# A spectral mixer with a gated FFN on one core: the head's chain, the weight sums and the order of the steps rewritten

## The chip, the cores and the metric

The kernel runs on one core of a Trainium2 chip. The time is device microseconds of one launch. The core has five engines that run side by side, each in its own program order, and wait for each other by semaphores: TensorE (PE: matmuls, with PEld for the loading of weights), VectorE (DVE), ScalarE (ACT), GpSimd (POOL) and SyncE (SP), whose queue issues most transfers.

## The reference

x is 2048 x 512, all in fp32, with F = 1376:

```python
xn = _layernorm(x, axis=-1)
s = irfft2(rfft2(xn) * (w_r + 1j * w_i))      # the spectral filter, over both axes
gate, up = xn @ W_gate, xn @ W_up
g = silu((relu(gate) * up) @ W_down)
return x + s * g
```

## The kernel before

All heavy products run on PE in fp16. Each fp32 operand is split into a high and a low fp16 part, and a product is three passes: high by high, high by low, low by high. Before a weight is split, it is scaled by a power of two, one for each group of its 128-column tiles (`csc`), which is found from the sum of its squares. The split of a tile is an ACT pass (high = scale x raw) and a DVE pass (low = scale x raw - high). x^T, the transposed normalised rows, is split in the same way (`xT`).

**Stages.** The 2048 rows are eight chunks of two row tiles ("chunk c" below; row tiles 0 and 1 belong to chunk 0). Rows are loaded, normalised, transposed on PE ("turned"; tiles `head`), and go two ways: through the FFN in four blocks of 512 rows (gate and up products `gu`, hidden values `h`, down products `dn`), and through the transform (`fold`, the stages `s1`, `s2`, `y`, `z`, and so on). The last stage adds x + s * g and stores.

**The head.** While the first rows are on their way, PE runs idle matmuls into a PSUM tile `small` (`keep_busy`). The first rows' path is `load_x` (one transfer for each row tile of chunk 0), `stats` (bn_stats and bn_aggr on DVE), `deviation` (one over the standard deviation: DVE adds the epsilon, ACT takes a root of the variance, DVE takes the reciprocal and corrects it in one Newton step), `normalise` (`xf`), `turn_row` (four PE transposes into PSUM, a copy `xTf`, the high part of `xT` and its low part). The products of the first two weight groups (`product` with c = 0, f < 2) for the first two row tiles are made straight from fp32 `xTf` and `raw` weights, without a split; all others wait for split weights. Both row tiles of chunk 0 turn into one PSUM tile `head0`.

**Scales.** `squares` runs an ACT pass over each weight tile with a sum, `group_scale` adds the sums over the partitions with a small PE product (into `small` or `sum3`, `sum4`, ...) and makes the scale on DVE. Groups 3 to 5 are pairs of tiles.

**Weight sums.** For the later blocks, five pairs of weight tiles are multiplied in a scheme with fewer products, which needs sums and differences of scaled gate and up weights. `weight_sums` reloads the raw weights (`rp`), scales them in place on ACT (20 passes), makes four differences of each pair on DVE or POOL, and splits the results into high and low parts (`wT`, `wgu`).

**What sets the order.** Each piece of work is registered by `step` or `either` (a choice of engine), in the order of the code, with a cost and a due time. A table `ORDER` lists the number of the step to issue next, so it sets the order within every engine's queue; a string `PLACE` picks the engine of each step with a choice, and a string `SLOTS` the buffer of each tile. All instructions go out through the helper `InOrder`, so that nearly every row of the profile has that helper's line, L167 (L169 in the changed kernel), and instructions are told apart by their tiles.

Lines that the change touches: the constants at L40 to L48, the tables from L67, `load_x` L346, `stats` L362, `deviation` L373, `turn_row` L510, `squares` L616, `group_scale` L626, `all_scales` L673, `weight_sums` L680.

Of the kernel before, what the change touches and what calls it, by code (L numbers as in the profile page):

```python
# [42 lines left out]
NORM, TURN1 = (('DVE', 'DVE'), ('DVE', 'ACT')), 'PE'  # L43
# [3 lines left out]
BUSY, LATE = 42, 0.4  # L47
# [98 lines left out]
def columns(c, i):  # L146

    return (slice(0, 256), slice(256, 384), slice(384, D)) if (c, i) == (NBL - 1, 3) else (slice(0, D),)


def fwidth(f):
    return P if f < TAIL else F - P * TAIL


def fast(c, n):
    return c >= NBL - int(FASTS[n])


class InOrder:
# [77 lines left out]
def dve(n):  # L237
    return .07 + n / 960
# [27 lines left out]
def kernel(ctx: ExitStack, tc: tile.TileContext, x, wg, wu, wd, wl, ew, sp, c_r, c_d, c_m, c_x, c_s, out):  # L266
# [92 lines left out]
    def x_names(c, i):  # L359
        return [(f"x{c}", 0 if c else i)]  # L360
# [1079 lines left out]
```

## Time and profile before

| what | value |
| --- | --- |
| three runs | 397.18, 396.06, 395.64 us; median 396.06 |
| profiled execution | 394.64 us, of which 392.9 are the span of the trace |
| PE, DVE, ACT, POOL busy | 383.3, 312.0, 265.4, 92.0 us |
| PE's clock as granted | full speed over the whole span |
| first real product on PE | 9.36 us from the span's start |
| last product on PE ends | 386.75 us |

In a row of the timeline stand the start, the duration, the engine, the helper's line, the operation with what it writes and reads (the buffer numbers left out), the shapes and the count of the instructions that the row joins, and in brackets how long the engine was idle before it and which engine's result ended that. In a row of a group stand the count, then the busy time in us and the mean duration in ns, then the idle time in front of its instructions. "issue" and engine names with a q are the engine's sequencer.

### The profile page before, as it was taken

The numbers are of one execution on the slowest core, as the hardware profiler recorded it, in microseconds if no ns is written. First come the engines' busy times: TensorE is split into PE (matmuls) and PEld (weight loads), VectorE is DVE, ScalarE is ACT, GpSimd is POOL, SyncE is SP. The second block draws the span as 40 slices with busy tenths as digits, with TensorE's granted clock in tenths as the row PEclk, the third lists the DMA queues.
The fourth block names the chain that finished last, engine by engine and source line by source line (L and its number), as shares of the span: only waits on it lengthen the run. The fifth ranks groups of instructions, "written<-read, shape, count | busy, mean of one in ns | idle before, by whom it ended". The sixth has DMA issues, their size and how long they took to land. (4 is left out here: it accounts for less than half of the span.)

```text
span 392.9 us, 9009 instructions
## 1 busy us (share of the span) xinstructions
PE 383.3 (98%) x3548; PEld 264.5 (67%) x3548; DVE 312.0 (79%) x575; ACT 265.4 (68%) x517; POOL 92.0 (23%) x85
## 2 busy tenths in 40 slices
PE   8999999999999989999999999999999999999993
PEld 6865544545678868546888787745678776887543
DVE  5899999889798797996675997467475976369995
ACT  4989998899998976527648566644557654475511
POOL 2100023210250324320206225031114030432340
PEclk9999999999999999999999999999999999999999
DMA  7995377966476776898865606838556007999997
GB/s 272 402 344 189 114 185 176 313 156 141 140 262 191 285 202 186 215 203 206 270 236 171 208 2 203 238 78 196 139 171 193 13 7 206 261 238 271 235 231 192
DMA packets 67835, 77.97 MB, mean 198 GB/s; under 512 B 29072, under 2 KB 40944, under 8 KB 67792
## 3 DMA queue, kind: packets, MB, share of 16 engines
q1 hardware_dynamic: 66352, 74.77, 65.5%
q0 software_dynamic: 1440, 2.62, 4.4%
q8 instruction: 28, 0.46, 0.5%
q14 instruction: 15, 0.12, 0.1%
HBM read 46.95 MB, written 26.76 MB: 188 GB/s over the span
## 5 line engine op out<-in xcount | busy, mean ns | idle before, releaser
L167 PE MATMUL dn<-wds,h 128*128 128x512 f16 (+2 forms) x528 | 119.0, 372 | 0.0
L167 PEld LDWEIGHTS <-wgu 128*128 128x128 f16 x960 | 93.0, 98 | 38.3 <-issue 3.4
L167 PEld LDWEIGHTS <-h 128*128 128x128 f16 (+1 forms) x594 | 54.5, 98 | 51.5 <-issue 2.2
L167 PEld LDWEIGHTS <-wT 128*128 128x128 f16 x540 | 52.2, 98 | 9.8 <-issue 1.9
L167 PE MATMUL gu<-xT,wgu 128*128 128x512 f16 (+1 forms) x240 | 48.1, 358 | 0.8 <-DVE xT L167 0.8
L167 PE MATMUL sb<-xS,wT 128*128 128x256 f16 x360 | 44.2, 273 | 0.1
L167 PE MATMUL sa<-xT,wgu 128*128 128x256 f16 x360 | 44.2, 273 | 0.0
L167 PE MATMUL sb<-xS,wgu 128*128 128x256 f16 x180 | 22.1, 273 | 1.2 <-DVE se L167 1.2
L167 PE MATMUL sc<-xS,wgu 128*128 128x256 f16 x180 | 22.1, 273 | 0.0
L167 PE MATMUL sc<-xT,wT 128*128 128x256 f16 x180 | 22.1, 273 | 0.0
L167 ACT ACTIVATE g<-dn,cdi 128x512 f32<-128x512 f32 (+1 forms) x16 | 10.6, 671 | 12.7 <-PE dn L167 12.5
L167 POOL TENSOR_TENSOR h<-sr,h 128x512 f16<-128x512 f32 x8 | 10.2, 1280 | 31.6 <-ACT h L167 31.6
L167 PE MATMUL gu<-xT,wgt 128*64 128x256 f16 (+1 forms) x144 | 17.0, 309 | 0.0
L167 DVE TENSOR_TENSOR t<-v,t 128x1024 f16<-128x1024 f32 x8 | 9.8, 1223 | 8.5 <-ACT t L167 8.5
L167 ACT ACTIVATE p<-pf 128x1024 f16<-128x1024 f32 x8 | 8.5, 1058 | 11.9 <-DVE pf L167 8.7
L167 POOL TENSOR_TENSOR h<-se,h 128x512 f16<-128x512 f32 x6 | 7.0, 1159 | 39.1 <-ACT h L167 38.9
L167 DVE TENSOR_TENSOR sc<-sb,sk 128x512 f32<-128x512 f32 x15 | 10.5, 697 | 7.0 <-PE sb L167 6.2
L167 DVE TENSOR_TENSOR sr<-sb,sr 128x512 f32<-128x512 f32 x15 | 10.3, 688 | 6.2 <-PE sb L167 6.1
L167 DVE TENSOR_TENSOR a<-y,a 128x1024 f16<-128x1024 f32 x8 | 9.8, 1222 | 6.6 <-ACT a L167 6.6
L167 DVE SCALAR_TENSOR_TENSOR wgu<-raw,csc,wgu 128x512 f16<-128x512 f32 x20 | 14.6, 747 | 0.4 <-ACT wgu L167 0.3
L167 ACT ACTIVATE sb<-sa 128x512 f32<-128x512 f32 x15 | 8.7, 582 | 8.6 <-PE sa L167 8.5
L167 DVE TENSOR_TENSOR se<-sb,sk 128x512 f32<-128x512 f32 x15 | 10.3, 689 | 5.1 <-PE sb L167 4.9
(227 smaller groups left out, 766.1 us busy)
## 6 DMA issues: line engine op xcount, KB each, us to landing
rw<-in_wl SPq DMA_DIRECT2D x8, 512.0 KB, 4.5
A_d<-t SPq DMA_DIRECT2D x16, 256.0 KB, 3.8
wt<-in_wl SPq DMA_DIRECT2D x8, 512.0 KB, 5.4
at<-A_d SPq DMA_DIRECT2D x8, 512.0 KB, 5.5
C_d<-t SPq DMA_DIRECT2D x16, 256.0 KB, 3.5
ct<-C_d SPq DMA_DIRECT2D x16, 256.0 KB, 7.2
xf<-in_x SPq DMA_DIRECT2D x6, 512.0 KB, 5.4
N_d<-xf SPq DMA_DIRECT2D x6, 512.0 KB, 4.0
```

Of the source, the lines that this page charges most:

```text
L167: return lambda *args, **kw: self.tc.keep_in_program_order(f(*args, **kw))
```

## The change

- **Row tile 0 in halves.** It is loaded as two transfers of 256 columns each, and its statistics are taken from each half and joined. Row tile 1 stays whole.
- **Root last.** The scale of a row is now made as: DVE adds epsilon and scales, DVE takes the reciprocal, ACT takes the root. The Newton step is gone, and so is the tile `epsilon`.
- **Own PSUM tiles.** Each row tile of chunk 0 turns into a PSUM tile of its own, `head0_0` and `head0_1`.
- **Idle matmuls.** `BUSY` goes from 42 to 30.
- **Shared scales.** Groups 3 to 5 get one scale for each pair of tiles, and one ACT pass over 1024 elements instead of two over 512 for the squares. Only the first two columns of the sums are then made.
- **No scaling pass.** The sums of a pair are made from unscaled weights, where two of the four differences multiply by the ratio of the gate's scale to the up weights' (`ratio`, made in `all_scales`); the splits then multiply by the scale. For the two pairs of tiles that lie in different groups, these instructions are cut by tile.
- **Order, engines, buffers.** All three tables are new. Of chunk 1, both row tiles are normalised on DVE (one was on ACT).

The core of the diff (the tables are left out):

```diff
-NORM, TURN1 = (('DVE', 'DVE'), ('DVE', 'ACT')), 'PE'
+NORM, TURN1 = (('DVE', 'DVE'), ('DVE', 'DVE')), 'PE'
...
-BUSY, LATE = 42, 0.4
+BUSY, LATE = 30, 0.4
...
+        for name, rows, cols in ((("x0", "left"), slice(0, 1), slice(0, D // 2)), (("x0", 0), slice(0, 1), slice(D // 2, D)),
+                                 (("x0", 1), slice(1, 2), whole)) if c == 0 else ((("x1", 0), slice(0, 2), whole),):
...
+            def half(k):
+                DVE.bn_stats(T["sth"][:, k, :], T["x0"][:, 0, D // 2 * k:D // 2 * k + D // 2])
+                if k:
+                    DVE.bn_aggr(T["mv0"][:, 0, :], T["sth"])
...
+            def run(at=at):
+                v = T[f"q{c}"][:, 0, at]
+                DVE.tensor_scalar(v, T[f"mv{c}"][:, at, 1], EPS, 1.0 / XS ** 2, op0=ALU.add, op1=ALU.mult)
+                DVE.reciprocal(T[f"q{c}"][:, 1, at], v)
+            step("DVE", .32, run, reads=[(f"mv{c}", i) for i in rows], writes=[(f"q{c}", 1, rows[0])], port=True)
+            step("ACT", .2, lambda at=at: ACT.activation(T[f"q{c}"][:, 2, at], T[f"q{c}"][:, 1, at], AF.Sqrt),
+                 reads=[(f"q{c}", 1, rows[0])], writes=[(f"q{c}", 2, i) for i in rows])
...
-        if i == 0:
-            tile_of(f"head{c}", "F", [P, 2, D], F32)
+        name = f"head{c}" + f"_{i}" * (c == 0)
+        if c == 0:
+            tile_of(name, "F", [P, D], F32)
+        elif i == 0:
+            tile_of(name, "F", [P, 2, D], F32)
...
+        if shared(g):
+            for i in range(2):
+                step("ACT", act(1024) + .12, lambda i=i: ACT.activation(wgu[g][:, 1, i], T[f"raw{g}_{i}"], AF.Square, accum_out=T[f"m{g}"][:, i:i + 1]),
...
+            DVE.tensor_mul(ratio[:, 0], csc[:, 0], csi[:, 1])
+            DVE.tensor_scalar(ratio[:, 1], ratio[:, 0], -1.0, None, op0=ALU.mult)
...
-                step("ACT", act(512) + .1, lambda part=part, f=f, i=i: ACT.activation(part(), part(), AF.Copy, scale=csc[:, i, f:f + 1]),
-                     reads=[f"p{g}"], writes=[(f"{raw}_{i}", j)])
...
-        minus((0, 0), (1, 0), (0, 0), G + U, t1)
-        minus((1, 0), (1, 1), (1, 0), U + [t1], t3)
-        minus((1, 1), (1, 1), (0, 0), G + U + [t1, t3], t2)
-        minus((0, 1), (0, 1), (1, 1), G + [t2], t4)
...
+        scaled((0, 0), 1, (1, 0), ALU.add, G + U, t1)
+        plain((1, 0), (1, 1), (1, 0), U + [t1], t3)
+        plain((1, 1), (1, 1), (0, 0), G + U + [t1, t3], t2)
+        scaled((0, 1), 0, (1, 1), ALU.subtract, G + [t2], t4)
...
+                for cols, f in cut:
+                    ACT.activation(to(0)[..., cols], of()[..., cols], AF.Copy, scale=csc[:, 1, f:f + 1])
...
+                        DVE.scalar_tensor_tensor(to(1)[at], of()[at], csc[:, 1, f:f + 1], to(0)[at], op0=ALU.mult, op1=ALU.subtract)
```

How the order moves is shown at three places: before, then now. The first is ACT's queue in the head, from the copy of the first turned row on (`wgu0`, `wgu1` and `wgu3` with `m` are squares of a weight group, `q1` the root for chunk 1).

```order
6 L167 ACTIVATE xTf0_240<-head0_215 128x512 [waits PE_49]
7 L167 ACTIVATE xT0_242<-xTf0_240 128x512 [waits Activation_49]
8 L167 ACTIVATE xTf1_250<-head0_215 128x512
9 L167 ACTIVATE wgu3_105,m3_253<-raw3_0_238 128x4x128 [waits DMAHW5_49]
10 L167 ACTIVATE q1_257<-mv1_228,epsilon_136 128x2 [waits DVE_49]
11 L167 ACTIVATE wgu3_105,m3_253<-raw3_0_238 128x4x128
12 L167 ACTIVATE wgu3_105,m3_253<-raw3_1_271 128x4x128 [waits DMAHW6_49]
13 L167 ACTIVATE wgu3_105,m3_253<-raw3_1_271 128x4x128
```

```order
5 L169 ACTIVATE xTf0_233<-head0_0_221 128x512 [waits PE_49]
6 L169 ACTIVATE xTf1_242<-head0_1_227 128x512 [waits PE_49]
7 L169 ACTIVATE xT0_255<-xTf0_233 128x512 [waits Activation_49]
8 L169 ACTIVATE wgu0_102,m0_216<-raw0_0_165 128x512 [waits DMAHW4_49]
9 L169 ACTIVATE wgu3_105,m3_271<-raw3_0_181 128x1024 [waits DMAHW6_49]
10 L169 ACTIVATE q1_280<-q1_280 128x2 [waits DVE_49]
11 L169 ACTIVATE wgu3_105,m3_271<-raw3_1_188 128x1024 [waits DMAHW7_49]
```

The root of chunk 1 reads what DVE wrote into `q1` rather than the variance `mv1`; one square of group 0 has moved behind the copies. The second place is PE's queue around the first products (`small` from `ones` is idle work).

```order
73 L167 MATMUL head0_215<-unit_101,xf0_181 128x128 [waits DVE_49,Pool_49]
74 L167 MATMUL head0_215<-unit_101,xf0_181 128x128 x3
75 L167 LDWEIGHTS ones_126
76 L167 MATMUL small_154<-ones_126 128x256
77 L167 MATMUL small_154<-m0_189,ones_126 128x2 [waits Activation_49]
78 L167 MATMUL head0_215<-unit_101,xf0_181 128x128 [waits DVE_49]
79 L167 MATMUL head0_215<-unit_101,xf0_181 128x128 x3
```

```order
55 L169 MATMUL head0_0_221<-unit_101,xf0_213 128x128 [waits DVE_49,Pool_49]
56 L169 MATMUL head0_0_221<-unit_101,xf0_213 128x128 x3
57 L169 MATMUL head0_1_227<-unit_101,xf0_213 128x128 [waits DVE_49]
58 L169 MATMUL head0_1_227<-unit_101,xf0_213 128x128 x3
...
65 L169 MATMUL gu0_0_1_250<-xTf0_233,raw0_1_161 128x128 [waits DMAHW3_49,Activation_49]
...
72 L169 MATMUL gu0_0_0_275<-xTf0_233,raw0_0_165 128x128 x4
73 L169 MATMUL sum3_299<-m3_271,ones_127 128x2 [waits PE_49,Activation_49]
74 L169 MATMUL gu0_1_303<-xTf0_233,raw1_1_195 128x128 [waits DMAHW0_49,PE_49]
```

The two turns stand next to each other, in tiles of their own, and the sum for group 3 still stands between the products of group 0 and those of group 1. The third place is DVE's queue while the weight sums are made (`rp`: sums in place; `wT`, `wgu`: their low parts; `wds`: the low parts of the down weights; `h16`: those of the hidden values).

```order
160 L167 TENSOR_TENSOR wT0_109<-rp0_0_673,wT0_109 128x2x512
161 L167 SCALAR_TENSOR_TENSOR wds_115<-wds_115,scd_123 128x512
162 L167 TENSOR_TENSOR h16_0_10_1077<-h32_0_10_960,h16_0_10_1077 96x512
163 L167 TENSOR_TENSOR rp1_0_898<-rp1_1_1013,rp1_0_898 128x512
164 L167 TENSOR_TENSOR rp1_1_1013<-rp1_1_1013 128x512
165 L167 SCALAR_TENSOR_TENSOR wds_115<-wds_115,scd_123 128x512
166 L167 TENSOR_TENSOR h16_0_7_1164<-h32_0_7_1130,h16_0_7_1164 128x512
```

```order
155 L169 SCALAR_TENSOR_TENSOR rp1_0_727<-rp1_0_727,ratio_117,rp1_1_887 128x512
156 L169 TENSOR_TENSOR h32_0_7_1107<-gu0_7_1_1051,r0_7_952 128x512
157 L169 SCALAR_TENSOR_TENSOR rp2_0_1002<-rp2_0_1002,ratio_117,rp2_1_912 128x512
158 L169 SCALAR_TENSOR_TENSOR wds_115<-wds_115,scd_124 128x512
159 L169 SCALAR_TENSOR_TENSOR wT1_110<-rp1_0_727,csc_122,wT1_110 128x2x512
160 L169 SCALAR_TENSOR_TENSOR wds_115<-wds_115,scd_124 128x512
161 L169 SCALAR_TENSOR_TENSOR wT0_109<-rp0_0_629,csc_122,wT0_109 128x2x128 x4
162 L169 TENSOR_TENSOR h16_0_7_1140<-h32_0_7_1107,h16_0_7_1140 128x512
```

More of the sums and of their low parts stand ahead of the low part of the hidden values' tile 7 than before.

More of the change, by code (lines that the diff above doesn't have):

```diff
@@ L152, in fwidth, with shared @@
     return P if f < TAIL else F - P * TAIL
+def shared(g):
+    return tuple(GROUPS[g]) in PAIRS
 def fast(c, n):
@@ L316 @@
     DVE.memset(md, 0.0)
-    epsilon = cpool.tile([P, 1], F32, name="epsilon")
-    DVE.memset(epsilon, EPS * 4.0 / XS ** 2)
     T = Plan(ROOM)
@@ L523, in run @@
                 PE.transpose(head()[:, cols], T[f"xf{c}"][:, i, cols], unit)
-        step("PE", .45, run, reads=[(f"xf{c}", i)], writes=[(f"head{c}", i)], due=HEADS[c])
+        step("PE", .45, run, reads=[(f"xf{c}", i)], writes=[(name, i)], due=HEADS[c])
         if c == 0:
@@ L617, in squares @@
         tile_of(f"m{g}", "m", [P, 4], F32)
+        if shared(g):
+            for i in range(2):
+                step("ACT", act(1024) + .12, lambda i=i: ACT.activation(wgu[g][:, 1, i], T[f"raw{g}_{i}"], AF.Square, accum_out=T[f"m{g}"][:, i:i + 1]),
+                     reads=[f"raw{g}_{i}"], writes=[*(("wgu", f, 1, i) for f in GROUPS[g]), (f"m{g}", 0, i)], lead=SQUARES)
+            return
         for j, f in enumerate(GROUPS[g]):
@@ L677, in run @@
             DVE.scalar_tensor_tensor(rho, csi[:, 0], 2.0 ** 14, csi[:, 1], op0=ALU.mult, op1=ALU.mult)
-        step("DVE", .35, run, reads=[f"p{g}" for g in range(len(GROUPS))], writes=["rho"], port=True)
+            DVE.tensor_mul(ratio[:, 0], csc[:, 0], csi[:, 1])
+            DVE.tensor_scalar(ratio[:, 1], ratio[:, 0], -1.0, None, op0=ALU.mult)
+        step("DVE", .6, run, reads=[f"p{g}" for g in range(len(GROUPS))], writes=["rho"], port=True)
     def weight_sums(n, due):
@@ L699, in minus, with plain @@
+        parts = [(slice(0, 2 * P), fs[0])] if alike else [(slice(j * P, j * P + P), f) for j, f in enumerate(fs)]
+        by = [f"p{next(k for k, q in enumerate(GROUPS) if f in q)}" for f in fs]
+        def plain(to, a, b, reads, name):
             both(512, lambda e: e.tensor_sub(B(*to), B(*a), B(*b)), reads, [name], due=due)
-        t1, t2, t3, t4 = ((t16, f"t{k}") for k in range(1, 5))
-        minus((0, 0), (1, 0), (0, 0), G + U, t1)
-        minus((1, 0), (1, 1), (1, 0), U + [t1], t3)
@@ L703, in weight_sums, with scaled, run @@
-        minus((1, 1), (1, 1), (0, 0), G + U + [t1, t3], t2)
-        minus((0, 1), (0, 1), (1, 1), G + [t2], t4)
-        for to, of, needs, k in ((slice(0, 2), lambda: T[f"{raw}_0"].rearrange("p (t k) f -> p t k f", t=2), [*G, t1, t4, t2], 0),
-                                 (slice(2, 3), lambda: B(1, 1).unsqueeze(1), [*U, t2, t4], 2)):
-            m = 512 * (to.stop - to.start)
-            step("ACT", act(m), lambda to=to, of=of: ACT.activation(wT[n][:, to, 0], of(), AF.Copy), reads=needs, writes=[(t16, k)], due=due + 2)
-            both(m, lambda e, to=to, of=of: e.tensor_sub(wT[n][:, to, 1], of(), wT[n][:, to, 0]), needs + [(t16, k)], [(t16, k + 1)], due=due + 4)
+        def scaled(to, sign, b, op, reads, name):
+            def run():
+                for cols, f in parts:
+                    DVE.scalar_tensor_tensor(B(*to)[:, :, cols], B(*to)[:, :, cols], ratio[:, sign, f:f + 1], B(*b)[:, :, cols], op0=ALU.mult, op1=op)
+            step("DVE", stt(512) + .13 * (len(parts) - 1), run, reads=["rho", *reads], writes=[name], port=True, due=due)
@@ L712, in weight_sums, with first, second @@
             o = P * (f - GROUPS[g][0])
-            to = lambda h, g=g, o=o: wgu[g][:, h, 1, 0:2, o:o + P]
-            of = lambda j=j: B(1, 0)[:, :, j * P:j * P + P]
-            step("ACT", act(256), lambda to=to, of=of: ACT.activation(to(0), of(), AF.Copy), reads=[*U, t3], writes=[("wgu", f, 0, 1)], due=due + 2)
-            both(256, lambda e, to=to, of=of: e.tensor_sub(to(1), of(), to(0)), [*U, t3, ("wgu", f, 0, 1)], [("wgu", f, 1, 1)], due=due + 4)
+            split.append((lambda h, g=g, o=o: wgu[g][:, h, 1, 0:2, o:o + P].unsqueeze(1), lambda j=j: B(1, 0)[:, :, j * P:j * P + P].unsqueeze(1),
+                          [*U, t3], ("wgu", f, 0, 1), ("wgu", f, 1, 1), 256, [(slice(0, P), f)]))
+        for to, of, needs, high, low, m, cut in split:
+            def first(to=to, of=of, cut=cut):
+                for cols, f in cut:
+                    ACT.activation(to(0)[..., cols], of()[..., cols], AF.Copy, scale=csc[:, 1, f:f + 1])
+            def second(to=to, of=of, cut=cut):
+                for cols, f in cut:
+                    for k in range(1 if len(cut) == 1 else of().shape[1]):
+                        at = (slice(None), slice(None) if len(cut) == 1 else slice(k, k + 1), slice(None), cols)
+                        DVE.scalar_tensor_tensor(to(1)[at], of()[at], csc[:, 1, f:f + 1], to(0)[at], op0=ALU.mult, op1=ALU.subtract)
+            step("ACT", act(m) + .1 * len(cut), first, reads=[*by, *needs], writes=[high], due=due + 2)
+            step("DVE", stt(m) + .13 * ((len(cut) - 1) * 2 * m // 512 - (len(cut) > 1)), second, reads=[*by, *needs, high], writes=[low], port=True, due=due + 4)
     def weights(f, i):
```

67 lines of the change are left out of this document (28 added, 39 removed), and 122 rows, old and new, of the table ORDER.

## Prediction

> **What bounds the kernel now.** I read the page first, then TensorE's waits, then its timeline at the two ends and where it waits, and only there the engines that it waits for.
>
> ```profile
> span 392.9 us, 9009 instructions
> PE 383.3 (98%) x3548; PEld 264.5 (67%) x3548; DVE 312.0 (79%) x575; ACT 265.4 (68%) x517; POOL 92.0 (23%) x85
> ```
>
> TensorE (PE) is busy for 98% of the span. A busy share alone proves little, so the next view is the list of all that PE waits for in the whole run: what waited, for whom, microseconds in total, times, the longest.
>
> ```profile
> PE sb L167 <- DVE se L167: 1.2, 1, 1.2
> PE small L167 <- DVE epsilon L167: 1.1, 1, 1.1
> PE gu L167 <- DVE xT L167: 0.8, 1, 0.8
> ```
>
> Three waits, 3.1 us. PE's timeline shows where real work begins and where the wait for xT lies (start, duration, what, count, and in brackets the idle time before it):
>
> ```profile
> 1.06 6.45 PE L167 MATMUL small<-ones 128*128 128x256 f16 x36 [1.06 <-DVE epsilon L167]
> 7.35 0.60 PE L167 MATMUL head<-unit,xf 128*128 128x128 f32 x4
> 8.04 0.63 PE L167 MATMUL head<-unit,xf 128*128 128x128 f32 x4
> ...
> 9.36 3.84 PE L167 MATMUL gu<-xTf,raw 128*128 128x128 f32 x32
> 13.15 0.39 PE L167 MATMUL sum<-m,ones 128*128 128x4 f32 x2
> ...
> 18.39 0.38 PE L167 MATMUL gu<-xT,wgu 128*128 128x512 f16 x1
> 19.58 2.55 PE L167 MATMUL gu<-xT,wgu 128*128 128x512 f16 x11 [0.82 <-DVE xT L167]
> ```
>
> The 36 matmuls into "small" are idle work. The first product starts at 9.36 us, and the last ends at 386.75 (quoted with the end, below). In between PE stands still for about 2 us of 377. So the order of other engines' work is worth something only in three places: how early PE's first product starts, how long PE waits on the way, and what follows its last product. The products themselves are the same in both programs.
>
> **The start.** VectorE (DVE) and ScalarE (ACT) lead up to 9.36 us:
>
> ```profile
> 3.55 0.70 DVE L167 BATCH_NORM_STATS2 st<-x 128x6 f32<-128x512 f32 x1 [2.52 <-DMA x<-in_x]
> ...
> 4.56 0.68 DVE L167 BATCH_NORM_STATS2 st<-x 128x6 f32<-128x512 f32 x1
> 5.28 0.18 DVE L167 BATCH_NORM_AGGREGATE mv<-st 128x2 f32<-128x6 f32 x1
> 5.38 0.13 DVE L167 RECIPROCAL q<-q 128x1 f32<-128x1 f32 x1
> ...
> 6.00 0.55 DVE L167 TENSOR_SCALAR xf<-x,mv,q 128x512 f32<-128x512 f32 x1
> ...
> 7.16 0.55 DVE L167 TENSOR_SCALAR xf<-x,mv,q 128x512 f32<-128x512 f32 x1
> 8.87 0.69 DVE L167 BATCH_NORM_STATS2 st<-x 128x6 f32<-128x512 f32 x1 [1.16 <-DMA x<-in_x]
> ...
> 10.39 0.18 DVE L167 BATCH_NORM_AGGREGATE mv<-st 128x2 f32<-128x6 f32 x1
> ...
> 10.68 0.69 DVE L167 TENSOR_TENSOR eo<-xf 128x516 f32<-128x516 f32 x1
> ```
>
> ```profile
> 4.49 0.29 ACT L167 ACTIVATE q<-mv,epsilon 128x1 f32<-128x1 f32 x1 [2.26 <-DVE mv L167]
> ...
> 8.71 0.60 ACT L167 ACTIVATE xTf<-head 128x512 f32<-128x512 f32 x1 [1.55 <-PE head L167]
> ...
> 10.35 0.62 ACT L167 ACTIVATE wgu<-raw 128x512 f16<-128x512 f32 x1
> 10.88 0.19 ACT L167 ACTIVATION_READ_ACCUMULATOR wgu<-raw 128x1 f32 x1
> ```
>
> Now the new order, step by step. Row 0's first half has half the bytes and lands by 3.55 at the latest. Statistics over half a row are not in the trace: each half costs between 0.35 (half of 0.70) and 0.70. I take 0.4, so row 0's mean is there at about 4.2 rather than 4.46. But in the new DVE order row 1's statistics (0.68 + 0.18) stand ahead of row 0's tail, to 5.2. Then come a tensor_scalar and the reciprocal (0.15 + 0.13), ACT's root (0.29) and two handovers, to about 5.95: xf of row 0 ends at 6.5, against 6.55 before. Halving the row gains nothing by itself. xf of row 1 follows without a chain of its own, at 7.05 against 7.71.
>
> The gain lies behind it. By the order, 27 idle matmuls stand ahead of the turn of row 0, not 36. The last of them run at about 0.11 each (12 matmuls of the same 128x256 take 1.47 in a row quoted below), so nine fewer end about 1.0 earlier, at 6.5 rather than 7.5, and they no longer delay row 0's turn: it runs from 6.6 to 7.2, not from 7.35. The copy xTf of row 0 began at 8.71, four hundredths after row 1's turn ended (8.04 + 0.63), since both rows lay in one tile. With a tile for each row it starts at 7.25 and ends at 7.85, and the first product starts at about 8.0: **−1.36** (0.9 to 1.7).
>
> **A new wait right behind it.** PE reaches the sum over group 3's squares when the products of group 0 are done: 8.0 + 3.84 + 0.25 = 12.1. That sum needs ACT's second square of group 3. In the new ACT order the root of the second pair of rows stands ahead of that square. Before, the root was taken straight from the variance and waited for nothing late; with the root last it waits for DVE's reciprocal, and in DVE's order that stands behind both statistics (they end at 10.57, set by the landing at 8.87, which does not move: the same megabyte is asked for ahead of it), a cast of a 512-column tile (0.4 to 0.7), the 0.69 of eo, and a tensor_scalar of 0.15. So the reciprocal ends at about 12.1, the root at 12.4, the square over 1024 (0.62 for 512, so about 1.05, and 0.19 to read the sum) at 13.6. PE waits from 12.1 to 13.6: **+1.5** (0 to 1.7). Queued on ACT behind that root are also group 1's squares; on PE all of group 1. Note how this ties the start down: if the first product comes later than 8.0, this wait shrinks by as much. The start's whole effect is set by 13.6 against the 13.15 at which PE took the sum before.
>
> **The wait for xT.** From 18.39 to 19.58 PE did one 512-column product, whose pace in the next row is 0.22, so it lost 0.97. In the new order the low half of xT that it waited for is written by DVE ahead of xf of the second pair, and by 13 us it is done. What is late next is group 0's split at about 16, ahead of PE's need at 18.8. **−0.97** (−0.97 to 0).
>
> **The wait at 146 us.** The row of PE behind it, and what DVE and GpSimd (POOL) did before:
>
> ```profile
> 147.04 1.47 PE L167 MATMUL sb<-xS,wgu 128*128 128x256 f16 x12 [1.19 <-DVE se L167]
> ```
>
> ```profile
> 143.70 2.62 DVE L167 TENSOR_TENSOR sx<-xf,xf 128x512 f32<-128x512 f32 x1
> ```
>
> ```profile
> 143.64 2.13 POOL L167 TENSOR_TENSOR sx<-sx,sx 128x1024 f16<-128x1024 f32 x1 [6.63 <-ACT sx L167]
> ```
>
> ```profile
> L167 DVE TENSOR_TENSOR rp<-rp,rp 128x512 f32<-128x512 f32 x12 | 8.2, 687 | 0.2
> L167 POOL TENSOR_TENSOR rp<-rp,rp 128x512 f32<-128x512 f32 x3 | 3.8, 1274 | 22.8 <-ACT rp L167 22.0 <-DVE rp L167 0.8
> ```
>
> A sum of two 512-column tiles takes DVE 0.69; beside POOL's 2.13 it took 2.62, so 1.9 were lost, and se, queued behind it, came 1.19 late. In the new order both low halves of sx of this block stand on DVE (about 1.4 more of its own work, two 512-column rows at 0.69), no POOL row is near, and an se stands between the sums, so that nothing longer than those 1.4 is ahead of one. **−1.19** (−1.19 to 0).
>
> **The weight sums and DVE's load.** The 20 scaling passes leave ACT:
>
> ```profile
> L167 ACT ACTIVATE rp<-rp,csc 128x512 f32<-128x512 f32 x20 | 13.6, 713 | 0.0
> L167 DVE SCALAR_TENSOR_TENSOR wgu<-raw,csc,wgu 128x512 f16<-128x512 f32 x20 | 14.6, 747 | 0.4 <-ACT wgu L167 0.3
> ```
>
> ACT's 13.6 us are no gain in themselves: PE never waits for ACT. What counts is DVE. Three sums and three low parts of 512 and 256 columns come from POOL (3 x 0.69 + 0.75 + 2 x 0.5 = 3.8); the ten sums and twenty low parts of splits become scalar_tensor_tensor, 0.747 instead of 0.687 (+1.8); and the pairs of unlike groups are cut by scale, 12 more instructions at an estimated 0.1 of fixed cost (+1.2). That is about +6.8. The new order also moves other steps from POOL to DVE: it has 21 rows fewer on POOL, and at POOL's 1.27 against DVE's 0.69 the rest of them is about +8; the shorter root gives back about 1. So DVE gets about 13 us more. How much room has it?
>
> ```profile
> 50.00:70.00 20.00, 20.00 (x116) 9.41 (x113) 18.93 (x39) 17.85 (x39) 5.48 (x4) 1.00 0.74 178
> 70.00:100.00 30.00, 30.00 (x187) 14.78 (x179) 27.93 (x50) 27.43 (x50) 3.54 (x3) 1.00 0.67 190
> 100.00:130.00 30.00, 30.00 (x271) 23.27 (x264) 25.00 (x49) 27.87 (x59) 9.00 (x8) 1.00 0.70 220
> ```
>
> The columns are length, then busy time of PE, its weight loads, DVE, ACT and POOL. DVE is idle for 1.1, 2.1 and 5.0 us of these 80. By the order, the weight sums stand just there, and at 70 to 90 us some 4 to 5 us more of DVE's work stands ahead of the same product's inputs than before, of which about 2 are idle time now. PE's new wait there is 0 at best and 3 at worst if nothing is given back. I take **+1.0**, one wait of the size of the two in the trace (0.97 and 1.19): part of DVE's idle time is waiting for ACT and PE, which a fuller queue uses, and there is less POOL beside it.
>
> [...]
>
> **The end.** PE's last products, then ACT's and DVE's last rows:
>
> ```profile
> 382.73 0.37 ACT L167 ACTIVATE g<-dn_3bb,cdi 128x128 f32<-128x128 f32 x1
> 382.77 3.98 PE L167 MATMUL dn<-wds,h 96*128 96x512 f16 x34
> ...
> 386.80 0.47 ACT L167 ACTIVATE g<-dn,cdi 128x256 f32<-128x256 f32 x1 [2.87 <-PE dn L167]
> 387.27 0.30 DVE L167 TENSOR_TENSOR sv<-sv,g 128x128 f32<-128x128 f32 x1
> ...
> 388.34 0.42 DVE L167 TENSOR_TENSOR xt<-xt,sv 128x256 f32<-128x256 f32 x1
> ```
>
> Before, the last product was the 256-column part of the last row, and DVE was late: of the 1.49 from the gate's end (387.27) to its own, its last two instructions need 0.85. From PE's end (386.75) to DVE's (388.76) it took 2.0. In the new order a 128-column part is last: 0.37 for the gate, 0.30 and about 0.30 for DVE, 1.0 in all if DVE is not late. **−1.0** (−1.3 to 0). The store behind it and the rest to 392.9 stay.
>
> **Sum.** −1.36 + 1.5 − 0.97 − 1.19 + 1.0 − 1.0 = −2.0. The profiled execution took 394.64, 1.4 under the median of 396.06; the difference of the two programs is taken to be the same for a median: 394.0. The other edits come to nothing: two small instructions on DVE for the ratios, fewer but longer squares on ACT (counted above where PE waits for one), and three transfers rather than two ahead of SP's weight loads (one short issue more).
>
> **Rivals.**
> 1. DVE becomes the bound in the weight sums. For it: 93% busy from 70 to 100 us, 13 us more to do, and PE waiting for low parts written by it alone. Against it: blocking by POOL falls. From 50 to 130 us there are 8.2 idle; about 10 of the 13 fall there. If only half of the idle time can be filled, PE waits about 6 rather than 1: 394.0 + 5 = 399, slower. It decides from about 5 of waiting; at 3 to 5 the kernel is unchanged, 396 to 398.
> 2. The wait for group 3's square does not come (the reciprocal or the cast is earlier than I count): 1.5 less, 392.5.
> 3. The end is not shortened, because DVE, without idle time over PE's last 25 us before, is late by its extra work: the 1.0 goes, and 0.5 of lateness comes, 395.5. No change.
> 4. DVE keeps up altogether, because the 21 rows that leave POOL had blocked it: half of each (21 x 0.64 = 13) would pay for all that DVE takes over. Then the 1.0 goes: 393.0. For it speaks the row of 2.62, against it the undisturbed 0.687. [...]
> 5. The start does not move, as row 0 is held by the transfer: then the new wait shrinks too, and the time is still about 394.
>
> **How the numbers follow.** A measurement of this kernel can tell about 0.5%, 2.0 us, from no change: below 394.1 is faster, above 398.0 slower. The forecast, with rival 5, gets 0.36 (0.24 of it below 394.1, the rest above it), rival 1 gets 0.25 (0.10 unchanged, 0.15 slower), rival 2 0.13 (faster), rival 3 0.14 (unchanged), rival 4 0.12 (faster). Faster 0.49, same 0.36, slower 0.15. The forecast's own range is 393.0 to 395.0; all terms at their good ends give about 391.2, and rival 1 up to its middle 397.8.
>
> **What would show it.** In the changed kernel: the first product at 8.0 ± 0.4; a wait of PE of about 1.5 before the products of group 1, released by ACT; none near 19 us; none on se near 146; DVE busy over 95% from 70 to 100 us, and PE's waits there in sum under 1.5; under 1.3 us from PE's last product to DVE's last instruction. Waits of PE on low parts (h, wT, wgu) of over 5 us in sum, or an end over 2.5, make the forecast wrong.

## The result and the profile after

The changed kernel takes 389.68 us (median of six runs, 389.42 to 392.88); the kernel before, on the same chip, 395.9 (394.82 to 397.18). The ratio is 0.9855, with a 95% interval of 0.9819 to 0.9891: it is faster by 1.5%, about 6 us, where 2 were forecast. The profiled execution took 389.53, 5.1 less than the one before (394.64); its span is 387.4, 5.5 less. The page's first lines, with the busy time of each engine:

```profile
span 387.4 us, 8968 instructions
PE 380.4 (98%) x3536; PEld 262.6 (68%) x3536; DVE 316.1 (82%) x599; ACT 254.3 (66%) x493; POOL 63.7 (16%) x63
```

DVE has 4.1 us more to do, not 13; ACT has 11.1 less and POOL 28.3 less. The list of all that PE waits for:

```profile
PE head L169 <- DVE xf L169: 1.6, 1, 1.6
PE small L169 <- DVE md L169: 1.1, 1, 1.1
PE sum L169 <- ACT wgu L169: 0.5, 1, 0.5
```

The waits for xT and se are gone. One wait for ACT is new, in the head, and so is one ahead of the first turn. PE's timeline at both ends:

```profile
7.20 1.06 PE L169 MATMUL head<-unit,xf 128*128 128x128 f32 x8 [1.63 <-DVE xf L169]
...
8.51 2.05 PE L169 MATMUL gu<-xTf,raw 128*128 128x128 f32 x16
...
13.10 0.38 PE L169 MATMUL sum<-m,ones 128*128 128x2 f32 x2 [0.53 <-ACT wgu L169]
...
18.10 4.13 PE L169 MATMUL gu<-xT,wgu 128*128 128x256 f16 x30
...
382.42 1.17 PE L169 MATMUL dn_3bb<-wds,h 128*128 128x128 f16 x18
```

What DVE did for the first two rows (row 0's halves, then row 1):

```profile
3.32 0.75 DVE L169 BATCH_NORM_STATS2 sth<-x 128x6 f32<-128x256 f32 x2 [2.30 <-DMA x<-in_x]
...
5.08 0.69 DVE L169 BATCH_NORM_STATS2 st<-x 128x6 f32<-128x512 f32 x1 [0.77 <-DMA x<-in_x]
...
6.50 1.00 DVE L169 TENSOR_SCALAR xf<-x,mv,q 128x512 f32<-128x512 f32 x2
```

Row 0's mean was there at 4.32. But the rest of its chain stands behind row 1's statistics, which waited for their load until 5.08, so `xf` starts at 6.50 (before, at 6.00). PE's rows cut the span into stretches: the first real product at 8.51, the first product of split operands at 18.10, PE's last product done at 383.59. Before, the same marks stood at 9.36, 19.36 (18.39 plus the 0.97 lost behind the one product) and 386.75. What stands behind PE's end, on ACT, DVE and SP's queue:

```profile
383.58 0.43 DVE L169 TENSOR_TENSOR xt<-xt,sv 128x256 f32<-128x256 f32 x1
383.63 0.37 ACT L169 ACTIVATE g<-dn_3bb,cdi 128x128 f32<-128x128 f32 x1 [0.54 <-PE dn_3bb L169]
384.03 0.29 DVE L169 TENSOR_TENSOR sv<-sv,g 128x128 f32<-128x128 f32 x1
384.35 0.29 DVE L169 TENSOR_TENSOR xt<-xt,sv 128x128 f32<-128x128 f32 x1
```

```profile
380.56 4.45 SPq L169 DMA_DIRECT2D out<-xt  x6
```

For comparison, SP's queue of the kernel before in the same place (start, duration and count of the issues of the last stores):

```profile
386.19 3.84 SPq L167 DMA_DIRECT2D out<-xt  x6
```

DVE now ends 1.05 after PE (384.64), not 2.01. SP's last issue ends 0.37 after DVE (385.01); before, 1.27 after it (390.03 against 388.76). From there to the end of the span it is 2.39, before 2.87. So the 5.5 us divide thus:

| stretch | before | after | difference |
| --- | --- | --- | --- |
| span's start to first real product | 9.36 | 8.51 | −0.85 |
| to the first split product | 10.00 | 9.59 | −0.41 |
| to PE's end | 367.39 | 365.49 | −1.90 |
| to DVE's end | 2.01 | 1.05 | −0.96 |
| to the end of the span | 4.14 | 2.76 | −1.38 |

The profile of the kernel before is short at its end: from PE's end to the span's end it took 6.15, and 7.1 to 7.9 in the other six profiles with the order of before. With the order of the changed kernel it took 3.81 here and 3.9 to 5.0 in the other twelve. So the end can be worth about 3 us, not 2.3; that may be a part of why the medians lie 6.2 apart and the two profiled executions 5.1.

The windows in which the weight sums are made (length, then busy time of PE, its weight loads, DVE, ACT, POOL) hold the surprise:

```profile
70.00:100.00 30.00, 30.00 (x157) 15.18 (x156) 28.76 (x49) 23.93 (x49) 0.00 (x0) 1.00 0.78 210
100.00:130.00 30.00, 30.00 (x282) 23.69 (x281) 28.39 (x57) 25.82 (x55) 1.42 (x2) 1.00 0.55 172
```

DVE is busier by 0.8 and 3.4, and PE stands still for none of the 60 us.

### The profile page after: what moved, and what is told of

Read it like the earlier page. It is cut to its first block, busy times and chain, and to the rows that moved or that the text cites. A ratio compares the mean times of both kernels' runs of the same rounds, so it can differ in the third digit from the quotient of the medians.

```text
span 387.4 us, 8968 instructions
## 1 busy us (share of the span) xinstructions
PE 380.4 (98%) x3536; PEld 262.6 (68%) x3536; DVE 316.1 (82%) x599; ACT 254.3 (66%) x493; POOL 63.7 (16%) x63
## 3 DMA queue, kind: packets, MB, share of 16 engines
q0 software_dynamic: 1440, 2.62, 4.3%
## 4 chain that ended last, share of the span: by engine, by line
PE 94%; DVE 2%; DMA 2%; ACT 1%; issue 0%; SPq 0%; POOL 0%; DVEq 0%
PE dn L169 27%; PE gu L169 17%; PE sb L169 15%; PE sa L169 10%; PE sc L169 10%; PE s L169 3%; PE z L169 3%; PE xx L169 3%; DMA x<-in_x 2%; PE y L169 2%; PE v L169 2%; DVE sv L169 1%; DVE xt L169 1%; PE dn_3b L169 1%; DVE st L169 0%
## 5 line engine op out<-in xcount | busy, mean ns | idle before, releaser
L169 DVE TENSOR_TENSOR sr<-sb,sr 128x512 f32<-128x512 f32 x15 | 10.3, 688 | 11.1 <-PE sb L169 11.0
L169 POOL TENSOR_TENSOR xs<-ee 128x256 f32<-128x256 f32 (+1 forms) x3 | 2.2, 731 | 98.2 <-DVE ee L169 51.9
L169 ACT ACTIVATE sq<-sc 128x512 f32<-128x512 f32 x15 | 8.9, 590 | 12.4 <-PE sc L169 11.5
L169 DVE TENSOR_TENSOR w<-xsp,w 128x1024 f32<-128x1024 f32 (+1 forms) x12 | 12.6, 1047 | 3.3 <-ACT w L169 1.6
```

Source lines behind the costliest of these rows:

```text
L169: return lambda *args, **kw: self.tc.keep_in_program_order(f(*args, **kw))
```

## The experiments

All times are medians on the same chip as runs of the kernel before, whose medians lay between 395.7 and 396.4; a single run is called one. What a run is "over the changed kernel" is taken against 389.68, which was measured at another time, so it is sure to some 0.7 us only.

### What paid for DVE's extra work

Two theories: DVE's waits for POOL (3.4 us from 50 to 160 us), and what its rows had lost beside POOL's (a sum of 0.69 took 2.62), turned into work; or ACT, relieved of its scaling passes, delivered earlier and so made room. First the change's largest single wait, undone in the kernel before. **One sum from POOL to DVE** (the low half of `sx` at 143.6 us, one letter of `PLACE`, P to D):

> The kernel before with one step moved from POOL to DVE: the low half of the first row sums of block 2 (1024 columns, 2.13 us on POOL at 143.6). If POOL's instruction blocked DVE, the DVE sum beside it falls from 2.62 to 0.69, DVE gains 1.9 and pays 1.3, and PE's wait of 1.19 at 147 shrinks to under 0.7 or goes; the span is shorter by 0.5 to 1.2. If DVE's load was the cause, 1.3 more work makes the wait longer, about 2.4, and the span 1.2 longer.

One run took 395.72. PE's and DVE's rows at that place:

```profile
143.77 0.68 DVE L167 TENSOR_TENSOR sx<-xf,xf 128x512 f32<-128x512 f32 x1
```

```profile
146.32 1.47 PE L167 MATMUL sb<-xS,wgu 128*128 128x256 f16 x12 [0.39 <-DVE se L167]
```

The 2.62 of DVE's sum became 0.68, and PE's wait fell from 1.19 to 0.39: the long row was POOL's doing. PE ended at 386.37, 0.38 earlier than in the profile before, but DVE at 389.45, 3.08 behind it. DVE had worked there without a listed wait since 359 us: with the order of before, its backlog sets the end, and what PE gains doesn't reach it.

**The reverse, in the changed kernel** (the same step from DVE back to POOL):

> The changed kernel with one step put back from DVE to POOL: the low half of the first row sums of block 2, 2.1 us on POOL, 1.22 on DVE. If blocking is what counts, a DVE instruction beside it takes 1.5 to 2.7 us instead of 0.68, DVE is no faster for losing the step, and PE gets a wait of up to 1. If load is what counts, DVE gets 1.2 us of room and PE waits for nothing, as now.

DVE's rows beside POOL's row, then POOL's:

```profile
141.78 0.68 DVE L169 TENSOR_TENSOR h<-sr,h 128x512 f16<-128x512 f32 x1
142.38 0.68 DVE L169 TENSOR_TENSOR se<-sb,sk 128x512 f32<-128x512 f32 x1
142.98 1.75 DVE L169 SCALAR_TENSOR_TENSOR wgu<-rp,csc,wgu 128x256 f16<-128x256 f32 x1
```

```profile
141.66 2.79 POOL L169 TENSOR_TENSOR sx<-sx,sx 128x1024 f16<-128x1024 f32 x1 [22.36 <-ACT sx L169]
```

The low part took 1.75 instead of 0.48 (its group in the changed kernel: ten in 4.7 us). DVE lost 1.27, and doing POOL's step itself costs it 1.21. So moving it is neutral for DVE. POOL's row was longer too, 2.79 instead of the 2.13 of the kernel before, and two of DVE's rows ran undisturbed beside its start. POOL's 0.66 more is about the 0.68 of `h`; the low part of `wgu` ended at 144.73, 0.28 after POOL's row; `se`, which reads `sb` from PSUM, took its 0.68 in between. That POOL was held up by `h` and the low part by POOL is read from these times; no run shows it by itself. No wait of PE appeared in the stage; the run's 392.01 came from the head (below).

**All six of POOL's steps of the weight sums to DVE, in the kernel before**, nothing else of the change:

```diff
-    "...DDDDPDPDDDPPDDDDDPDDPDDDD..."
+    "...DDDDDDDDDDDDDDDDDDDDDDDDD..."
```

> The kernel before, with GpSimd's six instructions of the weight sums (three sums and three low parts) moved to VectorE, 3.8 us of VectorE's time by the forecast's prices. Waiting theory: what VectorE took over in the changed kernel was free because VectorE had been waiting for, or was blocked by, those very instructions; then no new wait of PE appears here and the time is the same or up to 1 us lower. Relief theory: it was free only because ScalarE lost its scaling passes; here those stay, so 3.8 more on VectorE come out as 3 to 4 us later (399 to 400).

396.21 against 396.29 (ratio 1.0, 0.9979 to 1.0021): free. The group rows of that run; then, from the waits of DVE from 50 to 160 us in the kernel before, its wait for POOL, the longer of the two that make it up, and the same sum in this run:

```profile
L167 DVE TENSOR_TENSOR rp<-rp,rp 128x512 f32<-128x512 f32 x15 | 10.2, 687 | 1.4 <-ACT rp L167 1.1
L167 DVE TENSOR_TENSOR wT<-rp,wT 128x1024 f16<-128x1024 f32 x5 | 6.1, 1217 | 0.0
L167 DVE TENSOR_TENSOR wgu<-rp,wgu 128x256 f16<-128x256 f32 x10 | 4.1, 416 | 0.0
```

```profile
DVE rp L167 <- POOL rp L167: 3.4, 2, 2.6
```

```profile
103.29 0.69 DVE L167 TENSOR_TENSOR rp<-rp 128x512 f32<-128x512 f32 x1 [2.58 <-POOL rp L167]
```

```profile
102.66 0.69 DVE L167 TENSOR_TENSOR rp<-rp 128x512 f32<-128x512 f32 x1
```

Before, DVE waited 2.58 for a sum on POOL. That sum took 1.28 and could start only when ACT had scaled its input, for which DVE now waits 1.14 itself. When DVE makes the sum, its next one starts 0.63 earlier. The larger low parts fell from a mean of 1.335 in the kernel before to 1.217: there one of them took 1.80, beside a sum of POOL. DVE's five groups of the weight sums grew by 2.5 only (24.7 to 27.2), and its wait for `rp` shrank by 2.3 (3.4 for POOL before, 1.1 for ACT now). The six steps were worth nothing on POOL.

**ACT's scaling passes left out, in the kernel before.** The sums are then made of unscaled weights.

```diff
-step("ACT", ..., lambda part=part, f=f, i=i: ACT.activation(part(), part(), AF.Copy, scale=csc[:, i, f:f + 1]),
+step("ACT", ..., lambda: None,
```

> The kernel before, without ScalarE's 20 scaling passes in the weight sums (13.6 us of ScalarE); the sums are then made of unscaled weights, so this part of the computation is changed. PE's waits between its first product and its end add up to about 2 us, 1.2 of them at 146 us. Waiting theory: at most those 2 us come back, 394 to 396. Relief theory, alone: the same here, since PE waited so little; but VectorE should show more idle time from 70 to 130 us than the 7.1 of before, 10 or more.

395.91 against 396.29 (ratio 0.9992, 0.9972 to 1.0011). ACT's relief brought nothing by itself, and no room: DVE was idle for 6.5 us from 70 to 130 us (2.0 and 4.5), in the kernel before for 7.1.

**The same, with a dose of DVE's work** (larger low parts of `wT` written twice), and the dose alone in the kernel before:

> As the run without the scaling passes (that part of the computation is changed in the same way), and the larger low parts of wT written twice, 6.7 us more for VectorE, a dose that cost the kernel before 6.9. Relief theory: without the scaling passes VectorE has room, and the dose costs 0 to 3 over the run without it. Waiting theory: VectorE's room comes from POOL's side, nothing changes there, and the dose costs 5 to 7 again.

> The kernel before with the larger low parts of the weight sums written twice (the same values): 6.7 us more on DVE at 75 to 140 us, where it is idle for about 12 of 90 us, to hold against the changed kernel with as much more, which took about 6 us longer. If the kernel before had room and the change has used it up, this costs 0 to 2 us. If the room was gone before, as rival 1 of the prediction had it, it costs 4 to 6, and then the change cannot have added to the work that counts: it must have taken away about as much blocking by POOL as it brought work.

With the passes the dose cost 6.9 (402.89 against 395.99; ratio 1.0198, 1.0168 to 1.0228); without them 5.1 (401.04 against 395.91). Relief can have paid for a part of 1.8 of such a dose, and the intervals don't settle even that; the rows written twice also took 7.8 more in the first case and only 6.9 in the second.

**The dose in the changed kernel**, larger low parts twice, then all of them twice:

> The changed kernel with the larger low parts of the weight sums written twice (the same values again): about 7 us more on DVE between 70 and 160 us. DVE's busy share there is 94%, with 5.2 us idle of 90. If idle time can be filled, PE waits 0 to 2 and the kernel stays within 2 us of the changed one; if DVE is the bound there, as rival 1 of the prediction had it, it takes 5 to 7 us longer.

> The same with all low parts of the weight sums written twice: about 16 us more on DVE, three times its idle time from 70 to 160 us. PE must wait then: if DVE's idle time is the only room, about 10 us more; if the low parts were also made well ahead of their use (the room then is larger than the idle time), under 5.

395.77 (ratio to before 1.0009, 0.9986 to 1.0031), which is 6.1 over the changed kernel for 7.8 us of work, and 403.62 for 16, 14 over it. PE's waits with the smaller dose:

```profile
PE sum L169 <- ACT wgu L169: 2.0, 1, 2.0
PE dn L169 <- DVE h L169: 1.3, 1, 1.3
PE sb L169 <- DVE se L169: 1.2, 1, 1.2
```

So the rival that DVE becomes the bound stands just beyond the change: it had hardly any slack for 7.8 us, before or after. What it took over in the change came with the end of waits of about the same size (below).

**High parts twice on ACT** (14.4 us more for ACT by its busy time, in the changed kernel):

> The changed kernel with the high parts of the weight sums written twice on ACT (the same values): about 12 us more there, close to the 13.6 that the scaling passes took. ACT is idle for 22 of 90 us from 70 to 160. The prediction said that ACT's 13.6 us are no gain in themselves: then this costs 0 to 1 us. If ACT's place in the chain counts (a low part waits for its high part), DVE is pushed back by it and it costs 3 us or more.

398.28 (ratio to before 1.007, 1.0045 to 1.0094), 8.6 over the changed kernel. PE never waited for ACT in the stage; it waited 1.84 for `h` and 3.10 for a load (row below), and DVE waited 5.2 for ACT's halves of `wT`, against 0.5 in the changed kernel.

```profile
100.34 1.90 PE L169 MATMUL sc<-xS,wgu 128*128 128x256 f16 x11 [3.10 <-DMA xf<-in_x]
```

Behind this last wait PE's granted clock was 0.75 in the mean from 99 to 103 us and 0.82 from 103 to 107, together some 3.4 us at half, so not all of the 8.6 is waiting. An engine for which PE never waited held up DVE here. Taking ACT's work away was worth nothing here, adding to it cost.

### The end

**A 256-column part last in the changed kernel, a 128-column one last in the kernel before:**

```diff
-    return (slice(0, 256), slice(256, 384), slice(384, D)) if (c, i) == (NBL - 1, 3) else (slice(0, D),)
+    return (slice(0, 128), slice(128, 256), slice(256, D)) if (c, i) == (NBL - 1, 3) else (slice(0, D),)
```

(This is the edit of the changed kernel; in the other, the two lines change places.)

> The changed kernel with the last row's parts turned round: the last product, gate, product with s, sum and store are 256 columns wide, not 128. Two readings of the 1.38 us by which the stretch from DVE's last instruction to the span's end shrank (4.14 to 2.76). If the width of the last store sets it, the stretch goes back to about 4.1 and the span from 387.4 to about 389.2 (0.35 for the wider gate and sums, 1.4 for the store). If the queue of stores on SP did it (before, the last store was issued 0.9 after its data were ready; now at once), the stretch grows only by what 128 KB need over 64 KB, about 0.4, and the span to about 388.2.

> The kernel before with the last row's parts turned round, so that the last product and store are 128 columns wide and all else stays. If the width is what counted at the end, both gains show here: from PE's last product to DVE's last instruction about 1.3 instead of 2.0, and 2.8 instead of 4.1 behind it, the span 2 us shorter (390.9). If the order counted (DVE late behind three sums of 512 columns, SP behind the stores of those), DVE stays late and the store is still issued late: 0.3 to 0.8 shorter.

One run each. The wide part last (390.6) took 1.66 from PE's end to DVE's, 0.61 more than with the narrow one. From there to the span's end it took 2.92, and with the narrow part 2.76 here and 2.88 to 3.89 in eleven other profiles: no effect of the last store's width is seen. (The 0.4 expected for 64 KB more was an estimate; in the changed kernel's last 9 us, stores of 256 KB took 2.5 from issue to landing and those of 64 KB 1.5, 0.33 for each 64 KB.) The narrow part last in the kernel before (395.59) took 3.06 and 4.07: nothing gained. DVE's last rows there:

```profile
386.57 1.89 DVE L167 TENSOR_TENSOR xt<-xt,sv 128x512 f32<-128x512 f32 x3
...
388.38 0.29 DVE L167 TENSOR_TENSOR sv<-sv,g 128x128 f32<-128x128 f32 x1
388.58 0.62 DVE L167 TENSOR_TENSOR xt<-xt,sv 128x256 f32<-128x256 f32 x2
389.12 0.29 DVE L167 TENSOR_TENSOR sv<-sv,g 128x128 f32<-128x128 f32 x1
389.44 0.29 DVE L167 TENSOR_TENSOR xt<-xt,sv 128x128 f32<-128x128 f32 x1
```

PE ended at 386.67 and DVE worked without a break to 389.73. In the kernel before, not the width of the last part but DVE's order sets this stretch: there, the last sums of three rows come in one bunch (the row of three), and then the stores too, which SP issues one after the other. In the changed kernel they are spread, and SP issues each as it is ready. With the order of before, SP's last issue ended 0.76 to 1.45 behind DVE in all seven profiles; with the new one 0.35 to 0.37 in twelve of thirteen.

### The head

**The root of chunk 1 behind group 3's second square on ACT**, and **row 0's chain ahead of row 1's statistics**, **row 0 in one transfer**; all three in the changed kernel, the first two by moved numbers of `ORDER`:

> The changed kernel with one step moved on ACT: the root of chunk 1 behind the second square of group 3, not ahead of it. If ACT's queue behind DVE's reciprocal makes PE wait 0.53 for that square, the wait goes, and 0.3 to 0.5 are won, less what the later rows of chunk 1 cost (their turn may start 0.3 later). If the weights of group 3 land only then, the square starts no earlier than 11.9 and the wait stays at 0.5.

> The changed kernel with the head's order mended for row 0: its root and its normalised row stand ahead of row 1's statistics, and its turn and first product ahead of row 1's turn. Row 0's data are there at 3.9, so the first product should start at about 6.9 instead of 8.5. If the start of the first product is worth time, 1.5 us are won. If, as the prediction had it, the squares of group 3 set the start (ACT takes the second at 11.9 to 13.05 whatever PE does), PE's wait for that sum grows from 0.5 to about 2 and nothing is won: the sum at 13.1, products of split weights from 18.1.

> The changed kernel with row 0 loaded by one transfer, its statistics still from two halves. The halves' own worth: the first statistics start at 3.3 with halves and at about 3.6 without; row 1 lands at 5.1 with three transfers and by 4.6 with two (as before). Since row 0's root waits behind row 1's statistics, the whole load should bring the first product forward by about 0.4, not back; the sum of group 3 still comes at 13.1, so the span stays at 387.4 within 0.3. If the halves do what they are there for, the first product comes 0.3 later.

One run each: 390.74, 389.11, 389.71. The first product, what follows it, and PE's row of the sum for group 3; last, ACT's square with the root behind it:

```profile
7.10 1.16 PE L169 MATMUL gu<-xTf,raw 128*128 128x128 f32 x8 [0.69 <-ACT xTf L169]
8.10 0.60 PE L169 MATMUL head<-unit,xf 128*128 128x128 f32 x4
...
9.43 0.60 PE L169 MATMUL small<-ones 128*128 128x256 f16 x4
...
12.68 0.38 PE L169 MATMUL sum<-m,ones 128*128 128x2 f32 x2 [0.65 <-ACT wgu L169]
```

```profile
7.92 2.05 PE L169 MATMUL gu<-xTf,raw 128*128 128x128 f32 x16
...
13.39 0.38 PE L169 MATMUL sum<-m,ones 128*128 128x2 f32 x2 [1.41 <-ACT wgu L169]
```

```profile
11.87 1.06 ACT L169 ACTIVATE wgu<-raw 128x1024 f16<-128x1024 f32 x1 [0.64 <-DMA raw<-in_wu]
```

The first group is row 0 first, the second row 0 whole, the last row the late root. With the root out of its way, the square waits for its weights: in that run the landing sets it, not ACT's order. An earlier first product is mostly given back. With row 0 first it came 1.41 earlier, but row 1's turn and four idle matmuls now stand behind it (0.87 more up to the end of group 0), the wait is 0.12 longer, and the sum comes 0.42 earlier. With row 0 whole it came 0.59 earlier and the wait grew by 0.88. Loading row 0 in halves is worth nothing that one run shows.

**The sum for group 3 behind the first product of group 1** (`order.remove(97)`, put in again behind 498), and the same **with row 0 first and idle matmuls ahead**:

> The changed kernel, with PE's small sum for group 3 moved behind the first product of group 1, nothing else. If PE's wait in the head (0.5 to 1.9 by the run) costs what it lasts, and now and then the clock behind it, the time is 388.9 (0.5 to 1 less) and the six times lie within 1 us of each other. If the weights of group 1 land no earlier than those of group 3, PE waits for them instead and nothing is gained: 389.7.

> The changed kernel with row 0 ahead of row 1 as in the run before, and two steps more: four idle matmuls moved into the wait for the first turned row (there they cost nothing, where they stand now they hold up the second row's products by 0.5), and the sum for group 3 moved behind the first product of group 1, so that PE has work while ACT makes that square. First product at 7.1, no wait of PE for the sum if the weights of group 1 are there by 12, and products of split weights from about 17.0 rather than 18.1: 1 us less than the changed kernel, 388.7, some 1.8% under the kernel before. If the landing of the weights sets the head, PE waits for group 1's weights instead, and it is 0.4 at most.

390.14 (389.93 to 390.69; ratio 0.9863, 0.9839 to 0.9887) and 391.02 (389.71 to 392.48; 0.9876, 0.9852 to 0.99): neither beats the changed kernel. With the sum out of the way, PE waits for the next thing that lands:

```profile
13.11 1.13 PE L169 MATMUL gu<-xTf,raw 128*128 128x128 f32 x8 [0.86 <-DMA raw<-in_wu]
14.08 0.29 PE L169 MATMUL sum<-m,ones 128*128 128x2 f32 x2
14.95 1.09 PE L169 MATMUL head<-unit,xf 128*128 128x128 f32 x8 [0.58 <-DVE csc L169]
```

**The wait made longer**, by making the second square of group 3 twice, alone and with 20 idle matmuls ahead of the sum:

```diff
-lambda i=i: ACT.activation(wgu[g][:, 1, i], T[f"raw{g}_{i}"], AF.Square, accum_out=...)
+lambda i=i: [ACT.activation(wgu[g][:, 1, i], T[f"raw{g}_{i}"], AF.Square, accum_out=...) for _ in range(2 if (g, i) == (3, 1) else 1)]
...
+            for _ in range(20 if g == 3 else 0):
+                matmul(T["small"][:, 256:], w[:, 0:P], w, start=True, stop=True)
```

> The changed kernel, with ScalarE's second square of group 3 made twice, so that PE's wait in the head for its sum lasts about 1.2 longer (1.7 to 3 us, by the landing). If the wait costs only what it lasts: 390.9, and the clock stays 1.0. If a wait of over about 1.7 us in the head brings the granted clock down to half for some 3.4 us, as in two profiles here, then about 1.9 on top: 392 to 393, in most of the runs.

> The same, with 20 idle matmuls (about 2.1 us) ahead of the sum, so that PE runs through the wait. If it is the standing still that brings the clock down, the clock stays 1.0 here and the time is 390.5 to 391, about 2 under the other run. If the drop has another cause (the burst of the first products, the transfers), it comes here too, and the time is that of the other run or more.

392.58 (390.83 to 393.56) and 393.76 (393.13 to 394.5). PE's clock in the first (the third number from the end is the granted clock):

```profile
14.00:15.00 1.00, 0.53 (x4) 0.54 (x5) 0.19 (x2) 1.00 (x5) 0.00 (x0) 1.00 1.07 425
15.00:16.00 1.00, 1.00 (x8) 1.00 (x7) 0.90 (x5) 1.00 (x4) 0.00 (x0) 0.60 1.02 411
16.00:17.00 1.00, 1.00 (x7) 1.00 (x7) 1.00 (x3) 1.00 (x3) 0.00 (x0) 0.50 1.05 428
17.00:18.00 1.00, 1.00 (x6) 1.00 (x5) 1.00 (x2) 0.22 (x1) 0.00 (x0) 0.50 1.02 412
18.00:19.00 1.00, 1.00 (x9) 1.00 (x8) 0.05 (x1) 0.93 (x2) 0.00 (x0) 0.69 1.09 425
```

PE stood still for 2.13, and then the clock fell to half for some 3.4 us. The split products started at 21.11, 3.0 later than in the changed kernel: 1.6 for the longer wait and 1.64 for the clock, since from the sum to the first split product it took 6.64 instead of 5.00 (18.10 less 13.10), less 0.24 by which the first product came earlier. The second run missed its purpose: the idle matmuls write the tile `small`, which DVE still had to read, so PE waited 1.71 all the same, and the 20 matmuls (2.2) delayed the sum on top:

```profile
14.14 2.34 PE L169 MATMUL small<-ones 128*128 128x256 f16 x20 [1.71 <-DVE csc L169]
...
21.21 3.00 PE L169 MATMUL gu<-xT,wgu 128*128 128x256 f16 x25
```

Its clock stayed at 1.0, though, and with 3.9 us from the last product to the sum it reached the split products at 21.21, about where the run with 2.13 and half the clock did.

## Why the prediction was wrong, point by point

The direction was right and the size was not: −2.0 was forecast, −5.5 came in the profiled spans. By the steps:

- **The start, −1.36, and the new wait behind it, +1.5.** The mechanism was right, the sizes were off in this execution: −0.85 and +0.53. PE's 27 idle matmuls ended at 5.56, not at the forecast 6.5 (36 of them had taken 6.45, more than 0.11 each). Then PE waited 1.63 for `xf`, since row 1's load landed at 5.08 here and row 0's tail is queued behind row 1's statistics. In sister runs with the same head order where row 1 landed by 4.5, the first product started at 7.81 to 8.04, as forecast. The wait went with ACT's second square more than with the first product: the square started at 11.23 with the high parts twice (first product at 8.19, wait 0.16), at 11.92 here, and at 12.64 with the dose (7.81, wait 1.95), each time right behind the root, which waited for DVE, as forecast. The late root shows that without the root the landing of group 3's weights can take its place. The two terms came to −0.32 instead of +0.14.
- **xT, −0.97, and the wait at 146 us, −1.19.** Right; both are gone. The single move of one sum took away 0.8 of the second.
- **DVE's load, +1.0: the step that failed first.** No wait came. The tally of +13 counted POOL's work as DVE's at DVE's price and left out what DVE had lost to that work: waits for POOL of 3.4 us, and longer rows beside it (2.62 and 1.80 in two of them). DVE's busy time grew by 4.1 in all. The weight sums took 5.9 more (24.7 to 30.6), near the 6.8 forecast for them (the 0.1 in it for each of 12 more instructions was an estimate with no row behind it; by the groups of `wT` it was 0.13, for twelve low parts of 256 columns took 5.1 where two of 1024 and two of 512, at 1.283 and 0.745, would take 4.1); outside them DVE's busy time fell by 1.8, where about 7 more had been forecast. There some rows became shorter, as the sum of 2.62 became 0.68 when POOL's step beside it was gone: the low parts `h` from `se` took 7.1 for nine rows before and 7.1 for ten now. From 50 to 160 us DVE's listed waits fell from 12.3 to 5.1. The row that spoke against rival 4, twelve sums at an undisturbed 0.687 while POOL made three, was misread: two of POOL's three sums ran while DVE stood and waited for them (2.58 and 0.85), and the third held up a low part, not a sum (1.80 at 104.62, where one at 142.23 took 1.22). Rival 4, that DVE keeps up, came true; of its cause, the move of POOL's six steps alone is shown to be free, and ACT's relief alone is shown to bring nothing. That the two together made all of the room is argued, not shown, and the new order of DVE's own queue stands beside them untested: in it DVE does 7.5 us more from 50 to 160 us (96.2 to 103.6) and PE waits for none of it, while in the old order a dose of 7.8 cost 6.9.
- **"ACT's 13.6 us are no gain in themselves."** Right for taking them away (0.9992). But the reason given, that PE never waits for ACT, would also allow adding to ACT, and that cost 8.6: PE waits for DVE, and DVE for ACT (5.2 us there).
- **The end, −1.0.** Right, −0.96 in these two profiles; with the order of before DVE was 2.7 to 3.3 behind PE in the six others, so 2.0 was a low value. The reason, a narrow last part, was half of it (0.61 by the wide tail). The narrow part alone brought nothing to the kernel before. DVE had to come out of its backlog first.
- **"The store behind it and the rest stay": the second step that failed.** They gave −1.38. Of it 0.90 is SP's queue, whose last issue before ended 1.27 behind DVE and now 0.37. The other 0.48, from that issue to the span's end, is not traced to a row, and this stretch varies by as much between profiles of one order (2.39 to 3.06 with the changed kernel's tail and SP's last issue at most 0.37 behind DVE).
- **Not in the sum at all.** Between the first split product and PE's end, 0.7 more went than the wait at 146 us. PE's waits don't show it, and no run tells where it is.

The missing 3.5 are thus 1.0 (DVE), 0.5 (head), 1.4 (store) and 0.7 (open). The good ends of all terms add up to −5.16, or 390.9, not the 391.2 of the forecast; the median of 389.68 lies below even that, for the stretch behind DVE's last instruction and the open 0.7 stood in no term.

## What to carry to other kernels

When work goes from a slow helper engine to a busy one, set against its cost the waits of the busy engine for that helper and its rows that are long only beside it; here six steps, priced at 3.8 us, cost nothing. A dose test (some steps done twice) tells how much room an engine really has, better than its idle share: in the kernel before, the 7 us in which DVE was idle from 70 to 130 us bought 0.9 of a dose of 7.8. And a chain's end is only as early as the queues behind it (here SP's last issue came 1.27 behind DVE before, and 0.37 now): read the last issues of the store queue too, not only the compute rows.

## What the runs showed of the hardware

Three waits of PE of some 2 us cost 1.64 more here than they lasted. In three profiles a stand of 1.73 (the sum back on POOL), 1.95 (the dose in the changed kernel) and 2.13 us (the longer wait) ahead of the sum for group 3 was followed by about 3.4 us at a granted clock of 0.5; eight turns then lasted 1.91 or 1.92 instead of 1.04, and from the sum to the first split product it took 6.64 each time, not 5.00. In two others, behind a stand of 1.76 (the wide tail) and of 1.71 (the idle matmuls), the clock stayed at 1.0. So the length alone does not decide. Later in the kernel, a stand of 3.10 us (the high parts twice) had such a drop behind it, and so had, by the mean clock of 0.94 from 130 to 160 us, the 2.45 that PE stood there without the scaling passes and with the dose; the stands of 2.38 and 2.45 (the dose in the kernel before) and of 2.65 (all low parts twice) had none, with 1.0 in the stretches around them. What decides is not shown. Nor is it shown that the changed kernel's one run of 392.88 comes from this drop, for it has no trace; but its mean granted clock was 0.994, and 0.997 to 0.999 in the other five. With the longer wait, too, the run of 390.83 had 0.999 and the three of 392.49 to 393.56 had 0.996.
